# Three pieces of small TensorE work moved within a decode-attention loop: the softmax's row sum, the output gather and the query projection

## The chip, the cores and the metric

The kernel runs on one core of one Trainium2 chip. Its time is the device time of one launch in microseconds (us), and the figure compared is the median of several runs. Engines are called as the profile calls them: PE (TensorE matmuls; its weight loads are PEld), DVE (VectorE), ACT (ScalarE), POOL (GpSimd) and SP (SyncE, which issues every large DMA here). DVE, ACT, PE and SP each take their instructions in the order in which the program wrote them.

## The reference

Two rounds of the same pair are computed for a batch of 8 tokens of width 640: attention over a cache, then a dense layer with a ReLU, each on the layer-normed input and added to it.

```python
q = (x @ wq)                       # 8 x 32 heads x 128
scores = q . k_cache * 128**-0.5   # 4096 cached keys a head
p = softmax(scores)
x = x + (p . v_cache) @ wo         # attention, on layernorm(x)
x = x + relu(layernorm(x) @ w1) @ w2
# and both once more, with the same caches and weights
```

Every token has its own keys and values, 8 x 32 x 4096 x 128 in bfloat16 each, 268 MB for K and as much for V. Both rounds need all of them, so nearly all of the work is reading the caches once per round.

## The kernel before, in words

The unit of work is a *visit*: one round (called a layer here), one batch element, one pair of heads. There are 256 of them (`NV`), in the order of the list `visits`, which interleaves the two layers of neighbouring batch elements: 12 visits of layer 0 of the next element, then 16 of layer 1 of this one, then the last 4 of layer 0.

For one visit the K tile and the V tile of two heads are loaded, 2048 KB each, with the 4096 keys laid over 128 partitions. `score(i)` (L292) forms the scores: DVE multiplies the K tile with the query in 8 parts (L298, tile `prod`, three buffers, `PRODS`), and PE folds each part into one PSUM bank with two matmuls against the identity (L302, tile `s_ps`, two buffers). `reduce_s` (L311) finishes the sum on DVE. Two visits together make a softmax: `softmax_a` takes the row maximum and transposes it on PE (L317), `softmax_b` takes the maximum over the partitions on DVE (`hmx` L321, `diag` L325), spreads it by a matmul (L329), and ACT does four exponentials with their row sums (L338). `softmax_c` (L345) is the matmul that sums the row sums over the partitions, and `softmax_d` takes the reciprocal on DVE (L351). `attend(v)` (L362) is 16 matmuls of V with the probabilities, after which ACT copies the result to `o_sb` (L367). `gather_o` (L373) is four small matmuls that collect the output of the two heads into `oT_ps`; `scale_o` (L378, DVE) multiplies by the reciprocal; `project_o` (L386) is 10 matmuls with wo; `add_y` (L393, DVE) adds to the residual. `project_q` (L279) computes the queries of the next four visits, once in four visits, in the iteration before the one but next: 10 matmuls of 512 columns, and a copy on ACT (L284).

The main loop runs over i. Iteration i does `score(i)` and attends to visit v = i - 3. In even iterations (called even visits below) the softmax of the visits i - 2 and i - 1 is done too; `project_q(i + 2)` falls in every second even visit, that with i = 2, 6, 10 and so on. The dense layers and layer norms are a chain of small steps; `slot()` puts one of them into the loop at each of four places in an iteration, when there are any.

K and V tiles share one ring of three buffers (`RING`). SP issues V of the next visit (L269, `load_first`) as soon as the buffer of K(i) is free, that is when DVE's last product of `score(i)` is done, and K of visit i + 2 (L258, `load_second`) when the buffer of V(v) is free, that is when `attend(v)` is done. So at most two loads stand in the queue while the third buffer is being read. Two V tiles of each batch element (heads of `KEEP`) stay in buffers of their own from layer 0 to layer 1; there layer 1 loads no V.

The loop's body, as it was, ends in

```python
            slot(early=False)
            if blk is not None:
                softmax_c(blk)
            if v >= 0:
                gather_o(v, o_sb)
            if v - 1 >= 0:
                project_o(v - 1)
            slot(early=False)
            if i + 2 < NV and (i + 2) % GP == 0:
                project_q(i + 2)
```

Of the kernel before, what the change touches and what calls it, by code (L numbers as in the profile page):

```python
# [9 lines left out]
FP32 = mybir.dt.float32  # L10
# [3 lines left out]
AX = mybir.AxisListType  # L14
RING = 3
KEEP = 2
WARM = 0
NPART = 8
PRODS = 3
ENG = mybir.EngineType  # L20
# [11 lines left out]
def kernel(  # L32
# [12 lines left out]
    nc = tc.nc  # L45
    P = nc.NUM_PARTITIONS

    B, Sq, D = A_x.shape
    _, H, Sk, Dh = A_k_cache.shape
# [21 lines left out]
    ps = ctx.enter_context(tc.tile_pool(name="ps", bufs=1, space=bass.MemoryType.PSUM))  # L71
# [7 lines left out]
    wo_sb = wres.tile([P, H, D], BF16, name="wo_sb")  # L79
# [27 lines left out]
    ident_b = consts.tile([P, P], BF16, name="ident_b")  # L107
# [132 lines left out]
    NV = len(visits)  # L240
# [102 lines left out]
    def softmax_c(k):  # L343
        L_ps = blk_ps[k][:, P + 4 : P + 8]
        nc.tensor.matmul(  # L345
            L_ps, lhsT=ones_f, rhs=lrow2[k % 2].rearrange("p j h -> p (j h)"), start=True, stop=True
        )
# [22 lines left out]
    def gather_o(v, o_sb):  # L370
        oTp_tiles[v] = ps.tile([P, 2], FP32, name="oT_ps")
        for i in range(4):
            nc.tensor.matmul(oTp_tiles[v], lhsT=o_sb[:, i, :], rhs=dsel[:104, i, :], start=(i == 0), stop=(i == 3))  # L373
# [17 lines left out]
    def add_y(v):  # L391
        layer, b, hp = visits[v]
        nc.vector.tensor_tensor(out=xT[:, :, b], in0=xT[:, :, b], in1=y_tiles.pop(v), op=ALU.add)  # L393
# [10 lines left out]
    def load_first(i, v):  # L404
        if RING == 4 and i + 2 < NV:
            load_k(i + 2)
        if RING == 3 and 0 <= v + 1 < NV:
            load_v(v + 1)
# [9 lines left out]
    def slot(early=True):  # L418
        while early and chain and chain[0][0] == "D":
            chain.pop(0)[1]()  # L420
        if chain and chain[0][0] != "D":
            chain.pop(0)[1]()

    def warm():
        if WARM:
            w_ps = ps.tile([P, 512], FP32, name="w_ps", tag="q_ps")
            for _ in range(WARM):
                nc.tensor.matmul(w_ps, lhsT=ident_b, rhs=wo_sb[:, 0, :512], start=True, stop=True)

    LAG = 3  # L430
    o_parts = {}
    with tc.manual_schedule(engines={ENG.PE, ENG.DVE, ENG.Activation, ENG.SP}):
        load_wq(0)
        load_k(0)
        load_k(1)
        xT_ps = ps.tile([P, DC, B], BF16, name="ch_ps")
        for c in range(DC):
            nc.tensor.transpose(out=xT_ps[:, c, :], in_=x_bf[:, c * P : (c + 1) * P], identity=ident_b[:B, :B])
        nc.vector.tensor_copy(out=xT, in_=xT_ps)
        xln0 = consts.tile([P, DC, B], BF16, name="xln0")  # L440
        for _, step in ln_steps(0, B, xln0):
            step()
        for b in range(B):
            xlns[0, b] = (xln0, b)
        project_q(0)

        for i in range(NV + LAG):
            v = i - LAG
            new = i < NV
            blk = i // 2 - 1 if i % 2 == 0 and i >= 2 and i // 2 - 1 < NV // 2 else None  # L450
            if new:
                score(i)
                for f in late.get(i, []):
                    f()
            load_first(i, v)
            if v >= 0:
                o_sb = attend(v)
            load_second(i, v)
            if 1 <= i <= NV:
                reduce_s(i - 1)  # L460
            if blk is not None:
                softmax_a(blk)
            if v >= 0 and v % 2 == 0:
                softmax_d(v // 2)
            if v - 1 >= 0:
                scale_o(v - 1)
            if v - 2 >= 0:
                add_y(v - 2)
                if last_of[visits[v - 2][:2]] == v - 2:
                    chain += ffn_steps(*visits[v - 2][:2])  # L470
            slot()
            if blk is not None:
                softmax_b(blk)
            slot()
            slot(early=False)
            if blk is not None:
                softmax_c(blk)
            if v >= 0:
                gather_o(v, o_sb)
            if v - 1 >= 0:  # L480
                project_o(v - 1)
            slot(early=False)
            if i + 2 < NV and (i + 2) % GP == 0:
                project_q(i + 2)
            if new and v >= 0:
                warm()

        add_y(NV - 2)
        scale_o(NV - 1)
        project_o(NV - 1)  # L490
        add_y(NV - 1)
        chain += ffn_steps(*visits[NV - 1][:2])
        for _, step in chain:
            step()
        for c in range(DC):
            if c == 0:
                r_ps = ps.tile([B, DC, P], BF16, name="q_ps")
            nc.tensor.transpose(out=r_ps[:, c, :], in_=outT[:, c, :], identity=ident_b)
        xo = sm.tile([B, DC, P], BF16, name="xo", tag="prod", bufs=PRODS)
        nc.vector.tensor_copy(out=xo, in_=r_ps)  # L500
        nc.sync.dma_start(out=out.rearrange("b s (c p) -> (b s) c p", p=P), in_=xo)
# [30 lines left out]
```

## Time and profile before

| | |
|---|---|
| median of 6 runs | 2670.31 us (2661.88 to 2675.05) |
| the profiled execution | 2658.96 us, its span 2657.2 us |
| DVE busy | 1612.0 us, 61% |
| PE busy | 2044.6 us, 77% (2 x 15406 instructions) |
| ACT busy | 512.7 us, 19% |
| bytes moved | 1057.63 MB, mean 398 GB/s |
| mean granted TensorE clock | 0.839 |

PE's busy share counts pipelined matmuls whose ends are modelled, so it isn't PE at its peak. The DMA share is the mean busy share of the core's 16 DMA engines. A timeline row gives start, duration, engine, line, operation, output <- input with their sizes, how many, and in brackets how long the engine had been idle before it and what ended that. A row of windows gives, for a stretch of the span, the busy time of each engine with its number of instructions, the granted clock (PEclk), the DMA share and the GB/s.

### The profile page before, as it was taken

How to read it: one execution, taken by the hardware profiler on the slowest of the kernel's cores; microseconds unless marked ns; L12 is line 12 of the kernel's file. 1: busy time of each engine (PE TensorE's matmuls, PEld its weight loads, DVE VectorE, ACT ScalarE, POOL GpSimd, SP SyncE). 2: the span in 40 equal slices, each digit the busy share in tenths (PEclk: the TensorE clock that was granted, in tenths of full speed). 3: DMA queues.
4: the chain of work that ended last, by engine and by line, in shares of the span. 5: the costliest groups of instructions: out<-in, count | busy, mean ns of one | idle time of the engine just before them, and what ended most of it. 6: DMA issues, size and time to landing. Idle time of an engine off the chain costs nothing.

```text
span 2657.2 us, 38809 instructions
## 1 busy us (share of the span) xinstructions
PE 2044.6 (77%) x15406; PEld 868.7 (33%) x15406; DVE 1612.0 (61%) x3475; ACT 512.7 (19%) x1604; POOL 2.0 (0%) x15
## 2 busy tenths in 40 slices
PE   6667877787777977778687787778877787778786
PEld 2223332343323433234232343333333233333333
DVE  5446665666665666566566666666666565666663
ACT  1112211122111221122111121112211122112211
POOL 0000000000000000000000000000000000000000
PEclk8778888888888888888888888888888888888887
DMA  9999999999999999999999999999999999999997
GB/s 362 400 412 414 393 393 403 405 415 397 380 409 401 415 405 381 408 414 405 405 374 408 409 405 415 386 405 414 405 396 399 416 391 414 393 388 413 400 375 298
DMA packets 80839, 1057.63 MB, mean 398 GB/s; under 512 B 8128, under 2 KB 13968, under 8 KB 17168
## 3 DMA queue, kind: packets, MB, share of 16 engines
q1 hardware_dynamic: 80656, 1055.15, 96.5%
q8 instruction: 120, 1.97, 0.3%
q14 instruction: 63, 0.52, 0.0%
HBM read 1055.11 MB, written 0.01 MB: 397 GB/s over the span
## 4 chain that ended last, share of the span: by engine, by line
DMA 50%; PE 37%; DVE 5%; ACT 4%; issue 3%; SPq 1%; DVEq 0%; ACTq 0%
DMA K_sb<-in_A_k_cache_dram 37%; PE s_ps L302 24%; DMA V_sb<-in_A_v_cache_dram 12%; PE o_ps L362 5%; DVE prod L298 4%; PE q_ps L279 3%; ACT P_0_104 L338 2%; PE blk_ps L345 1%; PE ch_ps L210 1%; PE blk_ps L329 1%; PE y_ps L386 1%; DMA V_keep_22383<-in_A_v_cache_dram 1%; PE blk_ps L317 1%; ACT P_1_105 L338 1%; DVE hmx L321 1%
## 5 line engine op out<-in xcount | busy, mean ns | idle before, releaser
L298 DVE TENSOR_TENSOR prod<-K_sb,qb 128x1024 bf16<-128x1024 bf16 x2048 | 1304.3, 687 | 822.8 <-DMA K_sb<-in_A_k_cache_dram 551.6
L302 PE MATMUL s_ps<-prod,ident_b 128*128 128x512 bf16 x4096 | 1334.1, 461 | 161.6 <-DVE prod L298 154.2
L302 PEld LDWEIGHTS <-ident_b 128*128 128x128 bf16 x4096 | 455.6, 113 | 984.8 <-issue 824.0
L367 ACT CAST o_sb<-o_ps 104x512 bf16<-104x512 f32 x256 | 149.8, 585 | 1832.6 <-PE o_ps L362 1832.6
L311 DVE TENSOR_REDUCE S_sb<-s_ps 128x64 f32<-128x512 f32 x256 | 174.7, 682 | 0.2 <-PE s_ps L302 0.2
L362 PE MATMUL o_ps<-V_sb,P_0_104 128*8 128x512 bf16 x1920 | 132.4, 389 | 41.0 <-DMA V_sb<-in_A_v_cache_dram 40.5
L321 DVE TENSOR_REDUCE hmx<-blk_ps 2x2 f32<-2x128 f32 x128 | 35.7, 279 | 174.0 <-PE blk_ps L317 174.0
L362 PE MATMUL o_ps<-V_sb,P_1_105 128*8 128x512 bf16 x1664 | 114.3, 388 | 18.6 <-DMA V_sb<-in_A_v_cache_dram 18.6
L345 PE MATMUL blk_ps<-lrow_1_107,ones_f 128*128 128x4 f32 x128 | 31.2, 314 | 125.3 <-ACT P_1_105 L338 125.3
L373 PE MATMUL oT_ps<-dsel,o_sb 104*128 104x2 bf16 x1024 | 63.1, 165 | 78.2 <-ACT o_sb L367 76.8
L345 PE MATMUL blk_ps<-lrow_0_106,ones_f 128*128 128x4 f32 x128 | 27.2, 283 | 102.4 <-ACT P_0_104 L338 102.1
L373 PEld LDWEIGHTS <-o_sb 104*128 104x128 bf16 x1024 | 60.1, 113 | 132.5 <-ACT o_sb L367 132.3
L386 PE MATMUL y_ps<-oT,wo_sb 128*128 128x1 bf16 x2560 | 100.6, 164 | 0.3 <-DVE oT L378 0.3
L329 PE MATMUL blk_ps<-diag,ones_f 2*128 2x4 f32 x256 | 50.7, 266 | 63.0 <-DVE diag L325 60.8
L338 ACT ACTIVATE P_0_104<-S_sb,nmax 64x64 bf16<-64x64 f32 x256 | 93.4, 365 | 4.5
L338 ACT ACTIVATE P_1_105<-S_sb,nmax 64x64 bf16<-64x64 f32 x256 | 93.3, 365 | 4.5
L362 PEld LDWEIGHTS <-P_0_104 128*8 128x8 bf16 x2048 | 53.3, 86 | 117.8 <-issue 95.5
L386 PEld LDWEIGHTS <-wo_sb 128*128 128x128 bf16 x2560 | 83.9, 98 | 0.4 <-DVE oT L378 0.4
L362 PEld LDWEIGHTS <-P_1_105 128*8 128x8 bf16 x2048 | 50.4, 86 | 95.9 <-issue 73.7
L284 ACT CAST qb<-q_ps 128x512 bf16<-128x512 f32 x64 | 37.4, 585 | 179.5 <-PE q_ps L279 179.5
L345 PEld LDWEIGHTS blk_ps<-lrow_1_107,ones_f 128*128 128x128 f32 x128 | 25.6, 250 | 130.9 <-ACT P_1_105 L338 130.9
L279 PE MATMUL q_ps<-wq_sb,xln_130 128*64 128x512 bf16 x320 | 66.1, 569 | 2.7 <-DMA wq_sb<-in_A_wq_dram 2.7
(228 smaller groups left out, 805.5 us busy)
## 6 DMA issues: line engine op xcount, KB each, us to landing
K_sb<-in_A_k_cache_dram SPq DMA_DIRECT2D x256, 2048.0 KB, 12.7
V_sb<-in_A_v_cache_dram SPq DMA_DIRECT2D x224, 2048.0 KB, 9.9
wq_sb<-in_A_wq_dram SPq DMA_DIRECT2D x4, 1280.0 KB, 14.8
wo_sb<-in_A_wo_dram SPq DMA_DIRECT2D x4, 1280.0 KB, 20.9
w_sb<-in_B_w_dram SPq DMA_DIRECT2D x1, 2160.0 KB, 25.8
w_sb<-in_B_w_dram SPq DMA_DIRECT2D x1, 2080.0 KB, 19.2
V_keep_1459<-in_A_v_cache_dram SPq DMA_DIRECT2D x1, 2048.0 KB
V_keep_1550<-in_A_v_cache_dram SPq DMA_DIRECT2D x1, 2048.0 KB, 19.5
```

The source lines that it names most:

```text
L279: nc.tensor.matmul(q_ps[hh * HP : (hh + 1) * HP], lhsT=_free(xl[:, c, col : col + 1], [(0, HP)]), rhs=wv[:, c, g, :, hh, :], start=(c == 0 ...
L298: nc.vector.tensor_tensor(out=prod, in0=K[:, :, lo : lo + DW], in1=_free(q[:, lo : lo + DW], [(0, J), (1, DW)]), op=ALU.mult)
L302: nc.tensor.matmul(s_tiles[i], lhsT=ident_b, rhs=prod[:, :, k * RW : (k + 1) * RW], start=(part == 0 and k == 0), stop=(part == NPART - 1 ...
L311: nc.vector.tensor_reduce(out=S_tiles[k][:, j, :], in_=s_tiles.pop(i), axis=AX.X, op=ALU.add)
L321: nc.vector.tensor_reduce(out=hmx, in_=blk_ps[k][:2, :P].rearrange("n (h p) -> n h p", h=2), axis=AX.X, op=ALU.max)
L329: nc.tensor.matmul(gmax, lhsT=ones_f[:2, :], rhs=diag.rearrange("n j h -> n (j h)"), start=True, stop=True)
L338: nc.scalar.activation(out=P2[k % 2][r, j, :, hh], in_=S[r, j, :], func=ACT.Exp, bias=nmax[r, j, hh : hh + 1], scale=inv_sqrt_dh, accum_ou ...
L345: nc.tensor.matmul(L_ps, lhsT=ones_f, rhs=lrow2[k % 2].rearrange("p j h -> p (j h)"), start=True, stop=True)
L362: nc.tensor.matmul(o_ps[32 * c : 32 * c + 8, :], lhsT=P2[k % 2][:, j, 4 * g : 4 * g + 4, :], rhs=V[:, 4 * g : 4 * g + 4, :], start=(g < 4) ...
L367: nc.scalar.copy(out=o_sb, in_=o_ps[:104, :])
L373: nc.tensor.matmul(oTp_tiles[v], lhsT=o_sb[:, i, :], rhs=dsel[:104, i, :], start=(i == 0), stop=(i == 3))
L386: nc.tensor.matmul(y_tiles[v][:, c : c + 1], lhsT=wo_sb[:, 2 * hp + hh, c * P : (c + 1) * P], rhs=oT[:, hh : hh + 1], start=(hh == 0), sto ...
```

## The change

Nothing is added or removed but a constant (`WARM`, zero) and a helper that it had switched off. The same instructions are written in another order, and the line numbers behind the constant fall by one.

- `softmax_c` (row sum) of a pair goes from the end of the even iteration in which its exponentials are done to the next iteration, behind the folds of `score` and ahead of the V products of `attend`.
- `project_o(v - 1)` goes from the end of the iteration to just behind `scale_o(v - 1)`.
- `add_y` now adds visit v - 1 in the same iteration, behind `softmax_b`; it added visit v - 2 ahead of the first slot.
- `project_q` now comes before `gather_o`, and `gather_o` is last of all.
- There are three slots an iteration for the dense chain instead of four.

```diff
             load_first(i, v)
+            if v >= 0 and v % 2 == 0:
+                softmax_c(v // 2)
             if v >= 0:
                 o_sb = attend(v)
             load_second(i, v)
...
             if v - 1 >= 0:
                 scale_o(v - 1)
-            if v - 2 >= 0:
-                add_y(v - 2)
-                if last_of[visits[v - 2][:2]] == v - 2:
-                    chain += ffn_steps(*visits[v - 2][:2])
+                project_o(v - 1)
             slot()
             if blk is not None:
                 softmax_b(blk)
+            if v - 1 >= 0:
+                add_y(v - 1)
+                if last_of[visits[v - 1][:2]] == v - 1:
+                    chain += ffn_steps(*visits[v - 1][:2])
             slot()
-            slot(early=False)
-            if blk is not None:
-                softmax_c(blk)
-            if v >= 0:
-                gather_o(v, o_sb)
-            if v - 1 >= 0:
-                project_o(v - 1)
             slot(early=False)
             if i + 2 < NV and (i + 2) % GP == 0:
                 project_q(i + 2)
-            if new and v >= 0:
-                warm()
-
-        add_y(NV - 2)
+            if v >= 0:
+                gather_o(v, o_sb)
+
         scale_o(NV - 1)
```

PE at the end of an even visit with a query projection (i = 38; `lrow` holds the row sums, `wq_sb` and `xq` the weights and input of the projection, a "..." stands for further rows of the same operation), before:

```order
L317 MATMUL blk_ps<-ident_f,mrow 2x128
L329 MATMUL blk_ps<-diag,ones_f 128x4
L345 MATMUL blk_ps<-lrow_0_106,ones_f 128x4
L373 LDWEIGHTS o_sb
L373 MATMUL oT_ps<-dsel,o_sb 128x2
...
L386 MATMUL y_ps<-oT,wo_sb 128x1
...
L279 MATMUL q_ps<-wq_sb,xq 64x512
...
L302 MATMUL s_ps<-prod,ident_b 128x512
```

and now, from the output projection to the V products of the next visit:

```order
L385 MATMUL y_ps<-oT,wo_sb 128x1
L328 MATMUL blk_ps<-diag,ones_f 128x4
L278 LDWEIGHTS xq
L278 MATMUL q_ps<-wq_sb,xq 64x512
...
L372 MATMUL oT_ps<-dsel,o_sb 128x2
...
L301 MATMUL s_ps<-prod,ident_b 128x512
...
L344 MATMUL blk_ps<-lrow_0_106,ones_f 128x4
L361 LDWEIGHTS P_0_104
L361 MATMUL o_ps<-V_sb,P_0_104 8x512
```

The row sum stood between the maximum and the gather, ahead of 24 matmuls and of the next visit's folds; it now stands behind those folds. The projection stands directly behind the maximum.

DVE over the same even visit's end and the odd visit that follows, before:

```order
L321 TENSOR_REDUCE hmx<-blk_ps 2x2
L325 TENSOR_TENSOR diag<-ident_f,hmx 2x4
L298 TENSOR_TENSOR prod<-K_sb,qb 128x1024 x8
L311 TENSOR_REDUCE S_sb<-s_ps 128x64
L351 RECIPROCAL invL<-blk_ps 128x4
L378 TENSOR_TENSOR oT<-oT_ps,invL 128x2
L393 TENSOR_TENSOR xT<-xT,y_ps 128x5
L298 TENSOR_TENSOR prod<-K_sb,qb 128x1024 x8
```

and now:

```order
L320 TENSOR_REDUCE hmx<-blk_ps 2x2
L324 TENSOR_TENSOR diag<-ident_f,hmx 2x4
L392 TENSOR_TENSOR xT<-xT,y_ps 128x5
L297 TENSOR_TENSOR prod<-K_sb,qb 128x1024 x8
L310 TENSOR_REDUCE S_sb<-s_ps 128x64
L350 RECIPROCAL invL<-blk_ps 128x4
L377 TENSOR_TENSOR oT<-oT_ps,invL 128x2
L392 TENSOR_TENSOR xT<-xT,y_ps 128x5
L297 TENSOR_TENSOR prod<-K_sb,qb 128x1024 x8
```

In the odd visit the rows read alike, but the reciprocal now needs a row sum that PE does in this same visit, and the add reads the `y_ps` that PE writes in this same visit, behind the V products; it read that of the visit before.

More of the change, by code (lines that the diff above doesn't have):

```diff
@@ L16 @@
 KEEP = 2
-WARM = 0
 NPART = 8
@@ L422, in slot @@
             chain.pop(0)[1]()
[L424 to L428, printed above, removed]
     LAG = 3
```

## The prediction

> **What bounds the kernel now.** I read the page first, then SP's waits, then the timeline of single visits, then windows from visit to visit.
>
> ```profile
> span 2657.2 us, 38809 instructions
> q1 hardware_dynamic: 80656, 1055.15, 96.5%
> DMA 50%; PE 37%; DVE 5%; ACT 4%; issue 3%; SPq 1%; DVEq 0%; ACTq 0%
> ```
>
> The queue that loads the caches is busy for 96.5% of the span, and half of the chain that ended last is DMA. A kernel that only waited for data would show little else on that chain; here 37% of it is PE. So the loads are the bound, but something on PE decides now and then when a load may start. SP's waits say what releases the loads, and DVE's what it lacks:
>
> ```profile
> SPq L269 <- DVE prod L298: 1237.1, 203, 10.5
> SPq L258 <- DVE prod L298: 302.1, 50, 8.7
> DVE prod L298 <- DMA K_sb<-in_A_k_cache_dram: 551.6, 213, 7.0
> DVE prod L298 <- PE s_ps L302: 244.7, 450, 4.6
> ```
>
> V's issue (L269) waits for the last product of `score` (203 times). DVE in its turn waits mostly for K to land, but for 244.7 us it waits for PE to free a product buffer. If that delay makes a V issue so late that the queue runs dry, it costs time; otherwise nothing. The visit behind a query projection shows both:
>
> ```profile
> 430.66 0.38 PE L329 MATMUL blk_ps<-diag,ones_f 2*128 2x4 f32 x2 [0.56 <-DVE diag L325]
> 432.89 1.90 DVE L298 TENSOR_TENSOR prod<-K_sb,qb 128x1024 bf16<-128x1024 bf16 x3 [2.29 <-DMA K_sb<-in_A_k_cache_dram]
> 433.12 0.38 PE L345 MATMUL blk_ps<-lrow_0_106,ones_f 128*128 128x4 f32 x2 [2.08 <-ACT P_0_104 L338]
> 433.36 0.24 PE L373 MATMUL oT_ps<-dsel,o_sb 104*128 104x2 bf16 x4
> 433.46 0.39 PE L386 MATMUL y_ps<-oT,wo_sb 128*128 128x1 bf16 x10
> 433.78 2.12 PE L279 MATMUL q_ps<-wq_sb,xq 128*64 128x512 bf16 x10
> 435.83 5.01 PE L302 MATMUL s_ps<-prod,ident_b 128*128 128x512 bf16 x16
> 436.90 3.29 DVE L298 TENSOR_TENSOR prod<-K_sb,qb 128x1024 bf16<-128x1024 bf16 x5 [2.11 <-PE s_ps L302]
> 440.22 0.33 SPq L269 DMA_DIRECT2D V_sb<-in_A_v_cache_dram  x1
> 442.79 4.90 DVE L298 TENSOR_TENSOR prod<-K_sb,qb 128x1024 bf16<-128x1024 bf16 x8 [1.79 <-DMA K_sb<-in_A_k_cache_dram]
> ```
>
> K is there at 432.89 and DVE fills its three buffers. PE, in order, stands for 2.08 us behind the exponentials for the row sum, then does gather, output projection and query projection, and folds only from 435.83. DVE stands still for 2.11 us, and V is issued 7.33 us behind K's landing (440.22 - 432.89). Is that too late? Windows of one visit each, from landing to landing, with their V issues, tell:
>
> ```profile
> 432.89:442.79 9.90, 8.90 (x67) 3.53 (x68) 5.89 (x13) 1.34 (x4) 0.00 (x0) 0.83 0.91 361
> 295.13:305.03 9.90, 8.24 (x62) 3.69 (x63) 6.16 (x12) 0.81 (x3) 0.00 (x0) 0.71 0.94 364
> 336.88:346.77 9.89, 7.64 (x60) 3.06 (x58) 6.07 (x12) 0.58 (x1) 0.00 (x0) 0.75 1.01 417
> 301.42 0.33 SPq L269 DMA_DIRECT2D V_sb<-in_A_v_cache_dram  x1
> 337.62 5.79 PE L302 MATMUL s_ps<-prod,ident_b 128*128 128x512 bf16 x16 [0.38 <-DVE prod L298]
> 342.79 0.33 SPq L269 DMA_DIRECT2D V_sb<-in_A_v_cache_dram  x1
> ```
>
> The last two columns are DMA share and GB/s. Issued 7.33 us after landing the share is 0.91; at 6.29 (301.42 - 295.13) 0.94; at 5.91 (342.79 - 336.88) it is 1.01. So **the deadline for V's issue lies at about 6 us** behind K's landing. Visits behind a query projection miss it; the others mostly hold it.
>
> **The change part by part.** *The row sum off PE's way.* In the visit above, the spread of the maximum ends at 431.04. What PE then does before the folds: query projection 2.12 us and gather 0.24, no wait between (ACT's copy is long done), so PE is free at 433.4. `project_o`, 0.39 us, now lies ahead of the spread, inside the 0.56 us that PE idles there for DVE; without that cover it would cost its 0.39. The folds need the first product, done some 0.7 us behind K's landing, at 433.6. They start there instead of at 435.83: **2.2 us earlier**, and V's issue comes at 5.1 to 5.9 us, within the deadline. Where no projection stands (the other even visits), the folds came only some 0.3 to 0.5 us late behind row sum, gather and projection; there V was in time and nothing is won.
>
> *What the late issue costs.* There are 256 visits, so 64 groups of four, each with one query projection. Windows of whole groups:
>
> ```profile
> 400.12:649.21 249.09, 194.61 (x1532) 83.30 (x1524) 150.97 (x330) 50.48 (x155) 0.00 (x0) 0.85 0.98 406
> 767.10:974.01 206.91, 165.40 (x1306) 72.55 (x1302) 127.03 (x277) 43.35 (x131) 0.00 (x0) 0.83 0.98 406
> 1091.25:1296.12 204.87, 161.62 (x1298) 70.12 (x1297) 126.11 (x277) 43.13 (x131) 0.00 (x0) 0.87 0.99 409
> 190.99:231.21 40.22, 30.58 (x202) 12.01 (x199) 25.12 (x52) 6.17 (x21) 0.00 (x0) 0.82 1.00 420
> 2052.31:2091.84 39.53, 29.43 (x197) 11.28 (x194) 24.68 (x53) 6.14 (x20) 0.00 (x0) 0.87 1.00 420
> 364.12:400.12 36.00, 29.12 (x212) 11.59 (x214) 25.26 (x57) 6.77 (x23) 0.00 (x0) 0.91 0.92 361
> 2058.82 0.33 SPq L269 DMA_DIRECT2D V_sb<-in_A_v_cache_dram  x1
> ```
>
> The first three are 6, 5 and 5 groups, with dense steps among them: 660.87 / 16 = 41.30 us a group at 406 to 409 GB/s. The next two are single groups that ran without a gap, at 420 GB/s; in the one from 2052.31 V behind the projection happened to be issued at 6.51 us, the earliest of such visits that I found. Their 39.53 and 40.22 us are what a group takes when the queue doesn't run dry. Bounds of the saving: 0 and 41.30 - 39.53 = 1.77 us a group. I take 40.22, the slower one, since dense steps also stand in PE's way: 1.08 us. Of the 64 groups, 8 are those with kept V tiles (below), and 4 stand at the start with weight loads in the queue and are left at nothing: 52 x 1.08 = **56 us** (bounds 0 and 92).
>
> *Groups with kept V.* Eight groups load only six tiles, as that from 364.12: 36.00 us at 361 GB/s. There K is often there first, and the engines set the pace. They win the row sum's wait and the projection's delay, but lose by the new order on DVE:
>
> ```profile
> 1346.32 1.89 DVE L298 TENSOR_TENSOR prod<-K_sb,qb 128x1024 bf16<-128x1024 bf16 x3 [0.79 <-DMA K_sb<-in_A_k_cache_dram]
> 1348.64 5.40 PE L302 MATMUL s_ps<-prod,ident_b 128*128 128x512 bf16 x16
> 1353.97 1.07 PE L362 MATMUL o_ps<-V_keep_10745,P_1_105 128*8 128x512 bf16 x16
> 1354.11 1.88 DVE L298 TENSOR_TENSOR prod<-K_sb,qb 128x1024 bf16<-128x1024 bf16 x3
> 1356.14 4.37 PE L302 MATMUL s_ps<-prod,ident_b 128*128 128x512 bf16 x16
> 1356.77 3.10 DVE L298 TENSOR_TENSOR prod<-K_sb,qb 128x1024 bf16<-128x1024 bf16 x5 [0.77 <-PE s_ps L302]
> ```
>
> DVE's `add_y` now waits for `project_o` of the same visit, hence for the row sum (0.38) and the V products (1.07) ahead of it, and the next visit's products are queued behind `add_y`. Here they started at 1354.11, beside the V products; they would start at about 1356.0 and end at 1360.9 instead of 1359.87, **1.0 us lost**, in two odd visits a group. Against it stand 1.6 us from the row sum (K at 1346.32, its folds only at 1348.64 instead of 0.7 us behind it) and some 2 from the projection: 3.6 - 2 x 1.0, about 1.5 us net a group, 8 x 1.5 = **12 us** (bounds: nothing, and 36.00 x (1 - 361/420) = 5.1 us a group, 41 in all).
>
> *The same wait in the other odd visits* I cost at nothing:
>
> ```profile
> 450.09 0.38 PE L329 MATMUL blk_ps<-diag,ones_f 2*128 2x4 f32 x2 [0.56 <-DVE diag L325]
> 454.27 2.50 DVE L298 TENSOR_TENSOR prod<-K_sb,qb 128x1024 bf16<-128x1024 bf16 x4 [4.24 <-DMA K_sb<-in_A_k_cache_dram]
> 455.01 5.30 PE L302 MATMUL s_ps<-prod,ident_b 128*128 128x512 bf16 x16 [1.73 <-DVE prod L298]
> 460.24 1.07 PE L362 MATMUL o_ps<-V_sb,P_1_105 128*8 128x512 bf16 x16
> ```
>
> The folds end at 460.3; with row sum, V products and output projection DVE is free at about 462.5, 8.2 us behind K's landing, and the next K lands 9.9 us behind it. That cover, 1.7 us, is gone where V is late or K early; then the head start of three products (1.88 us) is what can be lost. K's own issue slips by the row sum's 0.38 us; with V's load, some 5 us (half of 9.9), ahead of it in the queue that doesn't show. The slots, three for four, move the dense steps into more visits and change no sum.
>
> *The clock.* With the row sum gone, PE idles from the gather, here at about 450.7 (450.09 + 0.38 and 0.24 for the gather), to the folds at 455.01 without a break; before, row sum, gather and projection broke that gap. Its folds already ran at half clock in such visits (the window from 336.88 has a mean clock of 0.75), and DVE then ended at 5.9 us, still in time, so I add nothing. The Trainium skill ("TensorE: Matmul & The Clock Gate", HAM oscillation — how this bites in real kernels) warns of idle gaps of TensorE above some 3.4 us, after which it runs at half rate again; that speaks against the change. By it every odd visit starts slow, as the window at 0.75 did, and the sum would stay at the deadline's edge: that is the first rival.
>
> Sum: 56 + 12 = 68 us. From the profiled execution's 2658.96 that leaves 2591. The median shown is 11 us above that execution, so against 2670.31 the forecast is **2602 us**.
>
> **The rivals.** *The clock eats part of it.* PE falls to half rate in each odd visit, and with any further delay V is issued at 5.9 to 6.3 us, on both sides of the deadline. A visit at 6.29 us moves 364 GB/s instead of 417, so 9.9 x (1 - 364/417) = 1.26 us lost. If about every third of the 104 odd visits of the 52 groups does that, 35 x 1.26 = 44 us are given back, and 24 of the 68 remain: 2646. For it: the clock of 0.71 in the visit from 295.13. Against it: 0.75 from 336.88 with no loss.
>
> *Nothing comes of it.* The gap is caught up within the group by the ring's slack, and 1.77 us a group is the spread of dense steps and DMA, not V's issue: within 8 us of 2670. Against it: 0.91 of share exactly in the late visits.
>
> *Slower: DVE tied to PE.* If V's products in odd visits regularly end later than the next K lands (more than 9.9 us behind the last one; from there each further microsecond of PE is one of DVE), the head start of three products is lost on the path. At 1.0 us as in the kept group, in 104 odd visits, it is +104 us, against 68 won: 2670 + 36 = 2706. For it: the folds at half clock end 6.5 us behind landing (337.62 + 5.79 - 336.88), and a V that lands late puts the V products later still. Against it: 213 of 256 scores wait for K, and V stands ahead of the next K in the queue, so a late V makes K late too.
>
> **How the numbers follow.** Chances: forecast 0.60, clock 0.20, nothing 0.09, DVE tied 0.11. The forecast's own range is 2560 to 2630: from twice the unknown part (68 + 42, the middle between 1.08 and 1.77 and a better kept group) to 40 us won. With the clock's 2646 and a margin for the runs' spread of 13 us, 8 times in 10 it lies in 2560 to 2656. A measurement here can tell about 0.3%, 8 us, from no change. Faster by more: 0.60 + 0.20 and a little of the third case, 0.82; within it 0.07; slower 0.11.
>
> **What would show it.** Right: the row sum's waits for ACT fall from PE's list, the folds in visits behind a query projection start within 0.9 us of K's landing, V is issued less than 6 us behind it, groups take about 40 us, and the DMA share rises to 0.98 or more. Wrong: DVE's waits for `y_ps` reach many tens of microseconds with K already landed; the clock falls below 0.8 and V's issues move beyond 6 us; or V's issues come early and the group still takes 41 us, which would mean that the deadline was not the cause.

## The result, and the profile after

| | before | after |
|---|---|---|
| median, us | 2669.06 (20 runs, 2660.67 to 2676.51) | 2589.93 (10 runs, 2574.15 to 2595.80) |
| ratio, 95% interval | | 0.970 [0.9683, 0.9718] |
| mean granted TensorE clock of the profiled execution | 0.839 | 0.849 |

The change saves 79 us, 3.0%. The forecast was 2602 us, so it was 12 us too slow, and inside its range.

The lines of the page of after that answer to those of before (span; the queue of the cache loads with packets, MB and share of the span; shares of the chain that ended last):

```profile
span 2585.3 us, 38646 instructions
q1 hardware_dynamic: 80656, 1055.15, 98.6%
DMA 61%; PE 31%; DVE 5%; issue 2%; SPq 1%; ACT 0%; DVEq 0%; ACTq 0%
```

The queue moves the same packets and bytes; it is busy for 98.6% of the span instead of 96.5%. It stood idle for 93 us before (3.5% of 2657.2) and does so for 36 us now (1.4% of 2585.3): 57 of the 72 us by which the spans differ. The other 15 us are fewer busy microseconds for the same bytes (2564 and 2549). On the chain ACT's 4% is gone, which was the row sum's wait for the exponentials. The list of waits of after says the same (total us, times, longest):

```profile
SPq L268 <- DVE prod L297: 1113.6, 203, 7.3
DVE prod L297 <- DMA K_sb<-in_A_k_cache_dram: 489.5, 235, 6.0
DVE xT L392 <- PE y_ps L385: 160.0, 129, 4.0
DVE prod L297 <- PE s_ps L301: 69.0, 383, 2.0
```

DVE waited 244.7 us for PE to free a product buffer; that is 69.0 now. In its place stands a wait of the add for `y_ps`, 160.0 us in 129 visits. Here is the visit behind the same query projection as in the prediction, in the timeline of after (start, us, engine, line, work, and in brackets the idle time before it with its releaser):

```profile
418.78 0.38 PE L328 MATMUL blk_ps<-diag,ones_f 2*128 2x4 f32 x2 [0.33 <-DVE diag L324]
419.09 1.27 PE L278 MATMUL q_ps<-wq_sb,xq 128*64 128x512 bf16 x10
420.30 0.25 PE L372 MATMUL oT_ps<-dsel,o_sb 104*128 104x2 bf16 x4
420.37 4.90 DVE L297 TENSOR_TENSOR prod<-K_sb,qb 128x1024 bf16<-128x1024 bf16 x8 [1.57 <-DMA K_sb<-in_A_k_cache_dram]
421.12 4.80 PE L301 MATMUL s_ps<-prod,ident_b 128*128 128x512 bf16 x16 [0.57 <-DVE prod L297]
425.30 0.33 SPq L268 DMA_DIRECT2D V_sb<-in_A_v_cache_dram  x1
425.76 0.28 PE L344 MATMUL blk_ps<-lrow_0_106,ones_f 128*128 128x4 f32 x2
425.97 1.07 PE L361 MATMUL o_ps<-V_sb,P_0_104 128*8 128x512 bf16 x16
427.40 0.16 DVE L392 TENSOR_TENSOR xT<-xT,y_ps 128x5 f32<-128x5 f32 x1 [1.10 <-PE y_ps L385]
430.27 1.90 DVE L297 TENSOR_TENSOR prod<-K_sb,qb 128x1024 bf16<-128x1024 bf16 x3 [2.70 <-DMA K_sb<-in_A_k_cache_dram]
```

The projection runs before K lands (420.37). The folds start 0.75 us behind it instead of 2.94, DVE makes its eight products without a stop, and V is issued 4.93 us behind landing instead of 7.33. The row sum (425.76) waits for nothing. The add waits 1.10 us for `y_ps`, and is done 2.7 us before the next K.

Where the time went, as windows of the two kernels, cut where the K of visits 15 and 252 lands. First the head and then all that is steady, before and then after (columns: span, busy us of PE, PEld, DVE, ACT, POOL, granted clock, DMA share, GB/s); behind each the sum over the eight stretches of five visits around a kept V:

```profile
0.00:190.99 190.99, 117.59 (x666) 47.21 (x667) 94.21 (x192) 25.85 (x83) 2.04 (x15) 0.80 0.97 390
190.99:2588.08 2397.09, 1881.76 (x14284) 798.72 (x14281) 1488.60 (x3210) 473.46 (x1481) 0.00 (x0) 0.85 0.98 401
sum 360.61, PE 301.43 PEld 124.65 DVE 245.95 ACT 67.93 POOL 0.00; mean PE 37.68 PEld 15.58 DVE 30.74 ACT 8.49 POOL 0.00
```

```profile
0.00:184.49 184.49, 119.49 (x682) 49.00 (x683) 95.12 (x194) 25.92 (x84) 2.04 (x15) 0.78 1.00 404
184.49:2517.60 2333.11, 1840.81 (x14280) 813.74 (x14278) 1508.28 (x3210) 472.22 (x1481) 0.00 (x0) 0.86 1.00 413
sum 337.07, PE 280.33 PEld 119.23 DVE 244.40 ACT 69.58 POOL 0.00; mean PE 35.04 PEld 14.90 DVE 30.55 ACT 8.70 POOL 0.00
```

| part | before, us | after, us | won | forecast |
|---|---|---|---|---|
| head, to visit 15 | 190.99 | 184.49 | 6.5 | 0 |
| steady visits with V loads (second row less the sum) | 2036.5 | 1996.0 | 40.4 | 56 |
| eight stretches with kept V | 360.61 | 337.07 | 23.5 | 12 |
| the tail, behind visit 252 | 69.1 | 67.7 | 1.4 | 0 |

So the sum was near (68 us forecast, 72 between the two spans), but its two terms are off in opposite directions. The experiments had to say which edit carries the gain, and why the kept stretches gave twice what was forecast.

### The profile page after: what moved, and what is told of

The parts are those of the page before. It is cut to its first block, busy times and chain, and to the rows that moved or that the text cites. A ratio compares the mean times of both kernels' runs of the same rounds, so it can differ in the third digit from the quotient of the medians.

```text
span 2585.3 us, 38646 instructions
## 1 busy us (share of the span) xinstructions
PE 2004.8 (78%) x15406; PEld 886.0 (34%) x15406; DVE 1632.9 (63%) x3475; ACT 511.3 (20%) x1604; POOL 2.0 (0%) x15
## 3 DMA queue, kind: packets, MB, share of 16 engines
q1 hardware_dynamic: 80656, 1055.15, 98.6%
## 4 chain that ended last, share of the span: by engine, by line
DMA 61%; PE 31%; DVE 5%; issue 2%; SPq 1%; ACT 0%; DVEq 0%; ACTq 0%
DMA K_sb<-in_A_k_cache_dram 57%; PE s_ps L301 25%; DVE prod L297 5%; PE o_ps L361 4%; DMA V_sb<-in_A_v_cache_dram 4%; SPq L91 0%; PE ch_ps L209 0%; SPq L98 0%; SPq L84 0%; PE q_ps L278 0%; PE blk_ps L316 0%; PE y_ps L385 0%; PE blk_ps L344 0%; PE ch_ps L189 0%; PE blk_ps L328 0%
## 5 line engine op out<-in xcount | busy, mean ns | idle before, releaser
L301 PE MATMUL s_ps<-prod,ident_b 128*128 128x512 bf16 x4096 | 1359.7, 468 | 445.0 <-DVE prod L297 437.9
L301 PEld LDWEIGHTS <-ident_b 128*128 128x128 bf16 x4096 | 467.5, 115 | 1250.0 <-issue 1102.2
L392 DVE TENSOR_TENSOR xT<-xT,y_ps 128x5 f32<-128x5 f32 x256 | 39.5, 154 | 160.0 <-PE y_ps L385 160.0
L385 PEld LDWEIGHTS <-wo_sb 128*128 128x128 bf16 x2560 | 91.2, 96 | 58.9 <-issue 57.1
L372 PEld LDWEIGHTS <-o_sb 104*128 104x128 bf16 x1024 | 45.0, 99 | 74.6 <-ACT o_sb L366 44.6
L328 PEld LDWEIGHTS blk_ps<-diag,ones_f 2*128 2x128 f32 x256 | 38.4, 187 | 48.4 <-DVE diag L324 48.4
L278 PE MATMUL q_ps<-wq_sb,xln_130 128*64 128x512 bf16 x320 | 46.4, 425 | 2.8 <-DMA wq_sb<-in_A_wq_dram 2.8
L337 ACT ACTIVATION_READ_ACCUMULATOR P_1_105<-S_sb,nmax 64x1 f32 x256 | 47.3, 185 | 0.0
L337 ACT ACTIVATION_READ_ACCUMULATOR P_0_104<-S_sb,nmax 64x1 f32 x256 | 47.2, 185 | 0.0
```

The costliest lines, as they stand in the source:

```text
L278: nc.tensor.matmul(q_ps[hh * HP : (hh + 1) * HP], lhsT=_free(xl[:, c, col : col + 1], [(0, HP)]), rhs=wv[:, c, g, :, hh, :], start=(c == 0 ...
L301: nc.tensor.matmul(s_tiles[i], lhsT=ident_b, rhs=prod[:, :, k * RW : (k + 1) * RW], start=(part == 0 and k == 0), stop=(part == NPART - 1 ...
L328: nc.tensor.matmul(gmax, lhsT=ones_f[:2, :], rhs=diag.rearrange("n j h -> n (j h)"), start=True, stop=True)
L337: nc.scalar.activation(out=P2[k % 2][r, j, :, hh], in_=S[r, j, :], func=ACT.Exp, bias=nmax[r, j, hh : hh + 1], scale=inv_sqrt_dh, accum_ou ...
L385: nc.tensor.matmul(y_tiles[v][:, c : c + 1], lhsT=wo_sb[:, 2 * hp + hh, c * P : (c + 1) * P], rhs=oT[:, hh : hh + 1], start=(hh == 0), sto ...
```

## The experiments

The theory: V's issue behind a query projection is late because PE folds late, and getting the row sum's wait and the projection out of the way of the folds is all that the change does. The rival: the gain comes from elsewhere (the earlier output projection, DVE's order, a faster clock).

**One part of the change alone.** Three kernels are the one before, each with one edit; a fourth is the changed one with the row sum put back at the end of the even iteration.

Row sum alone:

```diff
             load_first(i, v)
+            if v >= 0 and v % 2 == 0:
+                softmax_c(v // 2)
             if v >= 0:
                 o_sb = attend(v)
...
-            if blk is not None:
-                softmax_c(blk)
             if v >= 0:
                 gather_o(v, o_sb)
```

> The kernel before with the row sum alone moved behind the next visit's folds; gather, output projection and query projection stay at the end of the iteration in their old order. Theory (V's issue has a deadline of about 6 us behind K's landing, and only the visit behind a query projection misses it): PE is free 0.24 + 0.39 + 2.12 us after the spread of the maximum, about 0.9 us behind K's landing instead of 2.9; folds there start within 1 us of landing, and nearly the whole gain comes, 60 to 75 us. Rival (the early output projection, the add and the three slots carry the gain): within 10 us of before.

Query projection alone, ahead of the row sum's wait:

```diff
             slot(early=False)
+            if i + 2 < NV and (i + 2) % GP == 0:
+                project_q(i + 2)
             if blk is not None:
                 softmax_c(blk)
...
             slot(early=False)
-            if i + 2 < NV and (i + 2) % GP == 0:
-                project_q(i + 2)
```

> The kernel before with the query projection alone moved, to directly ahead of the row sum, so that it runs while ACT does the exponentials; the row sum keeps its place and PE still waits for ACT there in every even visit. Theory (deadline): the folds behind the projection start about 1.3 us behind K's landing instead of 2.9, V is issued at 5.7 to 6.4 us, on the deadline's edge: 45 to 65 us of gain. Rival (PE's wait for ACT at the row sum, 227 us in all in the kernel before, is what costs): it stays in all 128 pairs, and at most half of the gain comes, 35 us or less.

Output projection, add and the three slots alone:

```diff
                 scale_o(v - 1)
-            if v - 2 >= 0:
-                add_y(v - 2)
-                if last_of[visits[v - 2][:2]] == v - 2:
-                    chain += ffn_steps(*visits[v - 2][:2])
+                project_o(v - 1)
             slot()
             if blk is not None:
                 softmax_b(blk)
+            if v - 1 >= 0:
+                add_y(v - 1)
+                if last_of[visits[v - 1][:2]] == v - 1:
+                    chain += ffn_steps(*visits[v - 1][:2])
...
-            if v - 1 >= 0:
-                project_o(v - 1)
...
-        add_y(NV - 2)
```

> The kernel before with the output projection, the add and the start of the dense chain moved as in the change, and three slots; row sum, gather and query projection keep their old places. Theory (deadline): PE is 0.4 us less late behind a projection, 2.5 us instead of 2.9; V is still issued near 7 us, too late: 5 to 15 us of gain there, and 8 to 16 us lost in the groups with kept V by the add's wait; within 10 us of before. Rival (this part carries the gain): 40 us or more.

The changed kernel with the row sum back:

```diff
-            if v >= 0 and v % 2 == 0:
-                softmax_c(v // 2)
             if v >= 0:
                 o_sb = attend(v)
...
                 project_q(i + 2)
+            if blk is not None:
+                softmax_c(blk)
             if v >= 0:
                 gather_o(v, o_sb)
```

> The changed kernel with the row sum alone put back into its old iteration, behind the query projection and ahead of the gather. Theory (deadline): folds behind the projection start about 0.9 us behind K's landing, as in the changed kernel but for 0.2 us; the gain over before stays within 10 us of that of the changed kernel, 65 to 80 us. Rival (the wait at the row sum costs): 35 us or less.

The gather's move was not tried by itself.

| kernel | median, us | ratio to before [95%] | saved, us | queue busy | folds behind landing, behind a projection, us | kept stretches, us | other steady visits, us |
|---|---|---|---|---|---|---|---|
| before | 2667.81 | 1 | 0 | 96.5% | 3.11 | 360.6 | 2036.5 |
| output projection alone | 2661.98 | 0.998 [0.9963, 1.0006] | 6 | 96.6% | 2.75 | 367.2 | 2035.9 |
| query projection alone | 2621.27 | 0.985 [0.9794, 0.9902] | 47 | 97.8% | 1.50 | 344.9 | 2017.0 |
| changed, row sum back | 2607.27 | 0.978 [0.9751, 0.9818] | 61 | 98.0% | 1.22 | 348.8 | 2002.4 |
| row sum alone | 2588.91 | 0.972 [0.9678, 0.9760] | 79 | 98.4% | 1.50 | 339.9 | 1994.5 |
| changed | 2589.93 | 0.970 [0.9683, 0.9718] | 79 | 98.6% | 0.99 | 337.1 | 1996.0 |

The last three columns are of one profiled execution each; the folds are the mean over the steady visits behind a projection. The changed kernel's saving is against its own 2669.06. In the other kernels whose row sum is moved (row sum alone, the two smaller doses, the late add and the first filler, below) the kept stretches took 337.0 to 341.4 us, so some 4 us there can't be told from nothing.

**The row sum alone brings the whole gain**, as far as four runs can tell. Its page has ACT at 0% of the chain, and the row sum waits once:

```profile
span 2587.5 us, 38636 instructions
q1 hardware_dynamic: 80656, 1055.15, 98.4%
DMA 59%; PE 34%; DVE 5%; issue 1%; SPq 1%; ACT 0%; DVEq 0%; ACTq 0%
```

```profile
PE blk_ps L345 <- ACT P L338: 1.6, 1, 1.6
DVE prod L298 <- PE s_ps L302: 92.3, 360, 3.3
```

The output projection, the add and the slots alone can't be told from no change in the kernel's time: the row sum still stands in the way of the folds there, as its list of waits shows, and the folds behind a projection come at 2.75 us.

```profile
PE blk_ps L345 <- ACT P L338: 235.4, 113, 2.2
DVE prod L298 <- PE s_ps L302: 205.4, 403, 4.4
```

The projection alone brings some 47 us, and the row sum put back costs the changed kernel some 18 us (0.9784 against 0.970, intervals apart), where under 10 had been expected. That second one is a miss with a lesson. Both kernels get the projection off the folds, and both still let the row sum wait in front of them. The list of waits of the changed kernel with the row sum back:

```profile
PE blk_ps L344 <- ACT P L337: 175.2, 110, 2.1
```

In steady visits with no projection ahead of them (the odd ones behind the other even visits) the folds started 0.82 us behind landing before, 1.20 with the projection alone, 1.21 with the row sum back, and 0.75 in the changed kernel. In the mean of these visits K landed 0.50 us behind the end of the exponentials before, 0.29 us ahead of it with the projection alone and 0.66 us ahead of it with the row sum back. So once the late V is mended, K no longer lands behind the exponentials, and the same row sum that was nearly harmless there is now late for it. In the kept stretches it shows in one timeline (the row sum put back):

```profile
1317.07 1.87 DVE L297 TENSOR_TENSOR prod<-K_sb,qb 128x1024 bf16<-128x1024 bf16 x3
1319.58 0.39 PE L344 MATMUL blk_ps<-lrow,ones_f 128*128 128x4 f32 x2 [2.08 <-ACT P L337]
1319.92 5.30 PE L301 MATMUL s_ps<-prod,ident_b 128*128 128x512 bf16 x16
1320.55 2.72 DVE L297 TENSOR_TENSOR prod<-K_sb,qb 128x1024 bf16<-128x1024 bf16 x4 [1.61 <-PE s_ps L301]
```

K is there when DVE comes (no wait ahead of 1317.07), but the folds start 2.85 us later, and DVE stands for 1.61. In the changed kernel the same visit makes its eight products in one go (the last two rows below), with the folds 0.74 us behind the start. The first two rows are the visit before it, whose add does wait for `y_ps`, 1.10 us:

```profile
1301.33 0.17 DVE L392 TENSOR_TENSOR xT<-xT,y_ps 128x5 f32<-128x5 f32 x1 [1.10 <-PE y_ps L385]
1301.43 4.90 DVE L297 TENSOR_TENSOR prod<-K_sb,qb 128x1024 bf16<-128x1024 bf16 x8
1309.21 4.90 DVE L297 TENSOR_TENSOR prod<-K_sb,qb 128x1024 bf16<-128x1024 bf16 x8 [0.45 <-DMA K_sb<-in_A_k_cache_dram]
1309.95 4.80 PE L301 MATMUL s_ps<-prod,ident_b 128*128 128x512 bf16 x16 [0.65 <-DVE prod L297]
```

Of the 18 us, one profiled execution each puts 11.7 in the kept stretches (348.8 against 337.1) and 6.4 in the other steady visits.

**A dose of delay.** If it is the time of V's issue that costs, more work on PE ahead of the folds must bring the loss back. The changed kernel got projection matmuls once more ahead of the real ones, whose result then overwrites theirs: 6 of the 10, all 10 (two rounds), and three times all 10 (four rounds).

```diff
+        for c in range(5):
+            for hh in range(2):
+                nc.tensor.matmul(
+                    q_ps[hh * HP : (hh + 1) * HP], lhsT=_free(xl[:, c, col : col + 1], [(0, HP)]),
+                    rhs=wv[:, c, g, :, hh, :], start=True, stop=True,
+                )
         for c in range(DC):
```

(`range(3)` for the 6; `[k % DC for k in range(3 * DC)]` for the four rounds.)

> The changed kernel with 6 of the 10 query-projection matmuls done once more ahead of the real ones (their results are overwritten): PE gets some 0.7 to 1.3 us more work ahead of the folds behind a projection, nothing else is altered. Theory (a deadline near 6 us with little slack): V is issued there at 6 to 6.7 us, part of the visits miss it: 10 to 35 us slower than the changed kernel. Rival (the gain did not come from the time of V's issue): within 8 us of the changed kernel.

> The changed kernel with the whole query projection done twice (the first result is overwritten): 1.1 to 2.1 us more of PE ahead of the folds behind a projection, so that they come as late as in the kernel before. Theory (deadline): V is issued at 6.5 to 7.5 us there, 35 to 60 us of the gain are gone again, and only the groups with kept V keep theirs. Rival (the time of V's issue is not the cause): within 8 us of the changed kernel.

> The changed kernel with the query projection's 10 matmuls done four times (the first three results are overwritten). Doing them twice moved the folds behind a projection only from 0.99 to 1.72 us behind K's landing, because PE, kept busy, ran them at full clock and slack took part of it. Three times the extra work should move the folds to 3 to 4.5 us and V's issue to 7 to 8.5 us, later than in the kernel before. Theory (the time of V's issue decides): by the idle time that all runs so far show for such issues (0.6 us at 7.0 to 7.5, 0.9 at 7.5 to 8, 1.35 above 8), the gain is mostly gone: 45 to 95 us slower than the changed kernel. Rival (PE's work behind a projection does not matter): within 15 us of the changed kernel, as with twice.

| kernel | median, us | ratio to before [95%] | folds behind landing, us | last product behind landing, us | queue idle in such a visit, us |
|---|---|---|---|---|---|
| changed | 2589.93 | 0.970 [0.9683, 0.9718] | 0.99 | 5.25 | 0.06 |
| 6 more | 2592.34 | 0.973 [0.9708, 0.9747] | 1.34 | 5.44 | 0.16 |
| 10 more | 2594.82 | 0.974 [0.9717, 0.9753] | 1.72 | 5.70 | 0.23 |
| 30 more | 2651.71 | 0.994 [0.9914, 0.9957] | 3.56 | 7.29 | 0.95 |
| before | 2666.63 | 1 | 3.11 | 7.56 | 0.82 |

The last three columns are means over the steady visits behind a projection; idle is worked out from the packets of the cache queue, as the idle part of the 16 engines between 3 and 10.5 us behind landing. The first two doses missed what was expected of them (10 to 35, and 35 to 60 us): with 2 and 5 us lost they came out as the rival had it. But they delayed the folds by 0.35 and 0.73 us only, too little for a test. A round of 10 took 2.12 us in the timeline of before, but 1.27 us in that of after, and 30 matmuls take 5.11 us where the largest dose stands in one piece (its timeline):

```profile
2218.86 1.90 DVE L303 TENSOR_TENSOR prod<-K_sb,qb 128x1024 bf16<-128x1024 bf16 x3 [1.78 <-DMA K_sb<-in_A_k_cache_dram]
2218.93 5.11 PE L278 MATMUL q_ps<-wq_sb,xln 128*64 128x512 bf16 x30
2225.16 4.38 PE L307 MATMUL s_ps<-prod,ident_b 128*128 128x512 bf16 x16
2228.92 0.33 SPq L268 DMA_DIRECT2D V_sb<-in_A_v_cache_dram  x1
```

That dose puts the folds 6.30 us behind landing here, in a visit with a dense step ahead of it too, and 3.56 us in the mean. V is issued 10.06 us behind landing in this visit, the queue's share falls back to 96.6%, and 62 of the 79 us are lost. In the profiled executions the queue is idle for 36 us and busy for 2549 in the changed kernel, idle for 90 and busy for 2570 with this dose, and idle for 93 and busy for 2564 before. So the busy microseconds come back with the idle ones; why the same bytes take longer is not shown. The window of the visit above has a DMA share of 0.79:

```profile
2218.86:2232.25 13.39, 13.04 (x119) 6.34 (x117) 6.23 (x14) 1.77 (x6) 0.00 (x0) 0.87 0.79 307
```

With these and the other kernels, 13 traces in all, the queue's idle time in a steady visit stands against the time at which V is issued in it like this:

| V's issue behind K's landing, us | 4.5-5 | 5-5.5 | 5.5-6 | 6-6.5 | 6.5-7 | 7-7.5 | 7.5-8 | 8-8.5 |
|---|---|---|---|---|---|---|---|---|
| visits | 545 | 377 | 856 | 69 | 43 | 50 | 45 | 9 |
| idle, us a visit | 0.02 | 0.06 | 0.13 | 0.22 | 0.37 | 0.60 | 0.90 | 1.32 |

Nine further visits, eight of them with the largest dose, have their issue at 8.6 to 10.2 us and 1.5 to 3.6 us of idle time. There is a deadline, but no edge at 6 us: idle time begins at about 5.5 and grows by some 0.2 to 0.4 us for each half microsecond from 6.5 on.

**DVE's wait for the output projection.** In the changed kernel the add of the visit before was put back to where it did not wait (ahead of the output projection, two visits late):

```diff
                 scale_o(v - 1)
+            if v - 2 >= 0:
+                add_y(v - 2)
+                if last_of[visits[v - 2][:2]] == v - 2:
+                    chain += ffn_steps(*visits[v - 2][:2])
+            if v - 1 >= 0:
                 project_o(v - 1)
...
-            if v - 1 >= 0:
-                add_y(v - 1)
-                if last_of[visits[v - 1][:2]] == v - 1:
-                    chain += ffn_steps(*visits[v - 1][:2])
...
+        add_y(NV - 2)
```

> The changed kernel with the add to the residual put back by one iteration, so that DVE no longer waits for the V products and the output projection of the same visit; all PE moves stay. Theory (DVE's wait costs only where K is there early): 1.0 us in two odd visits of 8 groups, 5 to 20 us faster than the changed kernel, all of it in the groups with kept V. Rival (DVE's 160 us of waiting for the output projection lie on the path in the other groups too): 30 us or more faster.

2591.66 us, ratio 0.972 [0.9706, 0.9737]: the same as the changed kernel, where 5 to 20 us had been expected to come back. Two visits of a kept stretch tell why. Windows from the first product of one visit to that of the next, the changed kernel first, then that with the add put back:

```profile
1294.29:1301.43 7.14, 6.19 (x44) 2.51 (x43) 5.84 (x12) 1.38 (x4) 0.00 (x0) 1.00 1.01 420
1301.43:1309.21 7.78, 6.89 (x53) 2.86 (x54) 6.37 (x16) 0.85 (x3) 0.00 (x0) 1.00 0.93 364
```

```profile
1293.61:1299.53 5.92, 5.11 (x26) 2.05 (x29) 5.72 (x12) 0.51 (x1) 0.00 (x0) 1.00 1.00 426
1299.53:1308.54 9.01, 7.53 (x79) 3.29 (x70) 6.44 (x17) 1.99 (x6) 0.00 (x0) 1.00 0.98 376
```

Without the wait the first visit is 1.22 us shorter, and the second 1.23 us longer: 14.93 against 14.92 us. DVE starts earlier and then waits longer for the K behind the two, 1.34 us instead of 0.45. Over all eight stretches it is 339.0 us against 337.1.

**A warmer PE.** To raise PE's granted clock, the changed kernel got further matmuls of 512 columns behind the gather, whose result nothing reads (filler): five in each even visit without a projection; then five, and three, in all visits but those with a projection.

```diff
                 gather_o(v, o_sb)
+            if new and v >= 0 and i % 4 != 2:
+                w_ps = ps.tile([P, 512], FP32, name="w_ps", tag="q_ps")
+                for _ in range(5):
+                    nc.tensor.matmul(w_ps, lhsT=ident_b, rhs=wo_sb[:, 0, :512], start=True, stop=True)
```

(`i % 4 == 0` in the first one, `range(3)` in the last.)

> The changed kernel with 5 further matmuls of 512 columns on PE behind the gather of every even visit without a query projection, into a bank that nobody reads, to shorten PE's idle time ahead of the next folds. Theory (half clock in the next visit is hidden, V being issued at 5.9 us at the latest): the folds there run at a higher clock, V comes some 0.3 us earlier, and the time stays within 8 us of the changed kernel. Rival (the half clock eats part of the gain): 10 to 25 us faster.

> The changed kernel with 5 further matmuls of 512 columns behind the gather in every visit that has no query projection, odd and even, so that PE's clock does not fall between visits. In only one visit of four they took V's issue there from 5.3 to 5.0 us but the other even visits got colder, and the time stayed. Theory (the rest of the idle time belongs to V issues at 5.5 to 6 us, which come from the half clock): all issues near 5 us, idle time of the queue down by up to 15 us, 5 to 20 us faster than the changed kernel. Rival (the queue's rate is the bound, the clock is hidden): within 5 us.

> The same with 3 matmuls instead of 5. Theory: between the changed kernel and the one with 5, 0 to 15 us faster, if 3 are enough to hold the clock; if the clock falls as before, no difference. Rival: within 5 us.

Five in one visit of four: 2590.62 us, ratio 0.972 [0.9699, 0.9737]. Five in three of four: 2580.85, 0.968 [0.9655, 0.9709], at a clock of 0.899. Three: 2579.74, 0.969 [0.9661, 0.9713], at 0.873. The intervals of all three overlap with that of the changed kernel, [0.9683, 0.9718]. The last two save some 7 us more, each against its own runs of before, which these runs can't tell from nothing: it stays open whether a warmer PE is worth that much. The up to 15 us less of idle time that had been expected of five in three of four are not there: its queue is idle for 39 us (98.5% busy, span 2577.4 us), the changed kernel's for 36. Its single trace shows 19 us less in the steady visits (1977.3 against 1996.0) and 11 us more in the kept stretches (348.1 against 337.1), so a gain and a loss may stand behind the small sum. A large cost of the clock in the kernel's time these runs exclude.

## Why the prediction was right, step by step

**What bounds the kernel: right.** V's issue behind a query projection came too late for the queue. The queue's idle time in such a visit fell from 0.82 to 0.06 us; over the 44 of them among the steady visits that is 33 of the 40.4 us won there. With the lateness brought back by a dose of matmuls the loss comes back; a part that leaves the folds late (the output projection alone) wins nothing.

**The sum: near, in part by luck.** The steady term was 16 us too much, the kept stretches 11.5 and the head 6.5 us too little, and these nearly cancel.

**"The folds start 2.2 us earlier, and V's issue comes at 5.1 to 5.9 us": right.** 0.99 us behind landing in the mean over such visits instead of 3.11, and 4.93 us for the V in the quoted one. "Within 0.9 us" was a little strict.

**"The deadline for V's issue lies at about 6 us": roughly.** By the table above it is a slope from 5.5 us on, and at 6 to 6.5 us a visit loses 0.22 us, not the 1.26 that the first rival priced it at (9.9 x (1 - 364/417)). One window at a share of 0.94 was too little to place an edge, and the prediction's own rows spoke against it: in the group from 2052.31 V is issued at 6.51 us, and the group ran at a share of 1.00.

**"52 x 1.08 = 56 us": too much.** The three stretches of 6, 5 and 5 whole groups, in windows of after:

```profile
389.50:632.29 242.79, 190.48 (x1516) 85.50 (x1516) 153.61 (x329) 49.97 (x154) 0.00 (x0) 0.84 1.00 415
745.09:949.08 203.99, 159.26 (x1312) 72.80 (x1312) 128.30 (x277) 43.20 (x131) 0.00 (x0) 0.84 0.99 411
1061.68:1263.68 202.00, 160.79 (x1312) 72.74 (x1312) 128.44 (x277) 43.21 (x131) 0.00 (x0) 0.85 1.00 418
```

648.78 / 16 = 40.55 us a group, not 40.22: 0.75 us won instead of 1.08, or 39 us over 52 groups, close to the 40.4 of the split (197 visits). The step that failed is taking a single group at 420 GB/s for the mean; without a gap in the queue these move 411 to 418.

**"Where no projection stands ... nothing is won": nearly right against before, but not at the new pace.** The folds there started 0.82 us behind landing before and start at 0.75 now. But that was read off the trace of before, where K landed behind the exponentials. The kernel with the row sum back shows what the row sum's wait is worth once the projection is mended: some 6 us in the steady visits, and 12 in the kept stretches, where the prediction had priced it.

**"8 x 1.5 = 12 us" in the kept groups: half of the 23.5 measured.** The mis-sized term is the loss set against the gain: "1.0 us lost, in two odd visits a group". DVE's wait is there as drawn (1.10 us), but the kernel without it is no faster, since K is the next to be late. (In the old order it may have cost: with the output projection alone these stretches took 367.2 us against 360.6, one execution each.) Without that debit of 2.0 us a group the term is 3.6 x 8 = 29 us; the 23.5 lie between the two, nearer to it.

**"First 4 groups at nothing": wrong by 6.5 us** (190.99 against 184.49, DMA share 0.97 against 1.00). The DMA share rose there although the weight loads stand in the queue. With the row sum alone moved this stretch took 184.82 us, so that move wins it too; which of its visits gain stays open.

**"The clock ... I add nothing": right as far as the runs can tell, though PE does fall to half rate.** A visit of after whose folds come behind a longer gap (timeline), and the window from its landing to the next:

```profile
410.80 6.23 PE L301 MATMUL s_ps<-prod,ident_b 128*128 128x512 bf16 x16 [3.65 <-DVE prod L297]
415.98 0.33 SPq L268 DMA_DIRECT2D V_sb<-in_A_v_cache_dram  x1
410.05:420.37 10.32, 9.24 (x58) 3.70 (x58) 6.72 (x14) 1.70 (x7) 0.00 (x0) 0.71 0.99 398
```

After 3.65 us of idle the 16 folds take 6.23 us, at a granted clock of 0.57; in the visit quoted first, after 0.57 us of idle, they took 4.80 at a clock of 1.00. The window's clock is 0.71. V is still issued 5.93 us behind the landing at 410.05, the DMA share is 0.99, and what such an issue costs is 0.13 us by the table. The Trainium skill ("TensorE: Matmul & The Clock Gate", HAM oscillation — how this bites in real kernels) has such gaps bring TensorE back to half rate, and its advice is a loop without them. The trace agrees with the rule here, but raising the clock from 0.849 to 0.899 with filler brought nothing that could be told from zero in the kernel's time, and no less idle time of the queue: what ends last in these visits is the load.

**The rivals.** The clock's 2646 would have needed many V issues beyond 6 us: in the steady visits there were 46 of 172 before, and there are 6 now. The slower 2706 would have needed K landed while DVE waits for `y_ps`. That wait is there, 160.0 us of it, but in 195 of the 196 steady visits DVE's next products waited for K all the same, and in the kept stretches the add only moved the wait.

## What to carry to other kernels

Find the load whose issue is released late, and plot the queue's idle time against the time of its issue over many visits: that slope prices every edit ahead of it, where one window gives a false edge. A wait of an in-order engine belongs behind the work that is due first; moving that one wait was worth here as much as all five edits together, within what the runs can tell, and only one-edit kernels showed it. What the profile of before shows to be harmless is harmless at the pace of before: once the first late thing is mended, look at the next one with the new landing times.

## What the runs showed of the hardware

The same ten projection matmuls took 2.12 us in the visit quoted before and 1.27 us in that after. Over the kernel, one group of them in before, with the output projection alone moved, with the row sum alone moved, and in after (busy us, mean ns of one):

```profile
L279 PE MATMUL q_ps<-wq_sb,xq 128*64 128x512 bf16 x320 | 62.4, 541 | 0.0
```

```profile
L279 PE MATMUL q_ps<-wq_sb,xq 128*64 128x512 bf16 x320 | 62.9, 545 | 0.0
```

```profile
L279 PE MATMUL q_ps<-wq_sb,xq 128*64 128x512 bf16 x320 | 40.8, 385 | 0.0
```

```profile
L278 PE MATMUL q_ps<-wq_sb,xq 128*64 128x512 bf16 x320 | 41.6, 391 | 0.0
```

With PE waiting some 2 us for the exponentials ahead of them they are slow; with that wait moved away they are fast, in the old place as in the new. With the projection written ahead of the wait (the projection alone, and the row sum put back) the mean is 386 and 384 ns. The granted clock over the ten was 0.57 in the visit quoted before and 1.00 in that after. What in the visit brings the clock down just there was not tested. So one wait cost its own 2 us and most of another microsecond of slower matmuls, and matmuls added in that place later cost less than the profile of before made it seem.
